# Sliding-window attention and a feed-forward layer: fp32 to fp16 in the DMA in place of on the engines

## The chip, the cores and the metric

The kernel runs on one core of a Trainium2 chip. The metric is the device time of one execution in microseconds, as the median of repeated runs. Before the change it is 325.88 us (13 runs, 324.3 to 328.38). Five engines work side by side and wait for each other by semaphores: PE (matmuls), DVE (vector), ACT (activation), Pool, and SP, which here only issues DMAs. Sixteen DMA engines move the data.

## What is computed

Attention over 8 batches, 8 heads, 576 positions and 64 dimensions, with two kinds of mask, then a feed-forward layer over the 4,608 tokens:

```python
scores = matmul(q, k.T) / sqrt(64)
rel = pos[:, None] - pos[None, :]
mask_plain = (rel >= 0) & (rel < 32)                       # heads 0 to 3
mask_dil = (rel >= 0) & (rel < 128) & (rel % 4 == 0)       # heads 4 to 7
attn = softmax(where(mask, scores, -1e9))
x = (attn @ v), all heads of a token side by side          # 4608 x 512
h = x @ w_in                                               # 512 x 2048
out = max(0.01 * h, h) @ w_out                             # 2048 x 512
```

Inputs and output are fp32. The kernel computes with fp16 operands and fp32 accumulation.

## The kernel before

**Half batches and units.** The four heads of one kind of one batch are a half batch n (0 to 15; even n are plain, odd n dilated). Each has three units u = 3n + s: s = 0 and 1 are the two pairs of heads over the first 384 positions, s = 2 is both pairs over the last 192. In the dilated kind the positions are taken by their remainder modulo 4.

**An order written out by hand.** `PROGRAM` is a list of steps; the loop at L360 executes them in this order, and each engine keeps its own share of the order. Nothing is rearranged later. The letters:

- `lq:n:p` (`load_qk`, L138) loads q and k of half batch n, pair of heads p (`b` for both), to fp32 tiles `qf`, `kf`; `lv:n` (L155) loads v to `vf`; `lw:i:g` (L316) loads a fourth of w_in (i = 0) or of w_out (i = 1), 1 MB, to `wf`. All of these are issued by SP. For n < 5 (`NPE`) q and k come as 128 rows of 2,304 bytes per pair, for the others as runs of 256 bytes.
- `cq`, `cv`, `cw` convert what was loaded to fp16 tiles (`qh`, `kh`, `vh`, `w1`, `w2`) on DVE (`V`), Pool (`P`) or ACT (`A`). `cv` makes two operations: all 128 partitions, and then 32 partitions that get a copy of the 32 rows of the tile's last quarter, for windows that begin in the tile before.
- `B:n:p` (L202), for n < 5: 18 + 18 transposes of 64x64 on PE and two copies from PSUM to `qT`, `kT`. `T:n` (L197), for the others: transposes by DMA.
- `S:u` (L241): scores of a unit into the one PSUM tile `sps`, then an exponential on ACT. `S:u:b` first adds a mask bias by two matmuls against an identity (L246); `S:u:m` doesn't, and `M:u` (L263) multiplies by a 0/1 mask on DVE instead.
- `D:u` (L272): sums (`den`) and values (`o`) on PE, then 1/sum, either by two activations on ACT (`l`) or by a reciprocal on DVE (`r`), and the product with it into the ring `xT` on DVE. With `p` its PSUM tiles come from the four-tile pool that the feed-forward uses as well.
- `I:c:j` (L334): four matmuls of the first feed-forward product for a chunk of 384 (or 192) tokens and one of 16 groups of columns, and the leaky ReLU on ACT. It needs `xT` of all heads for the chunk: units 0, 1, 3, 4 for chunk 0. `O:t:g` (L343): four matmuls of the second product for 128 tokens; after g = 3 the result is copied by ACT and stored by a DMA that ACT issues.
- `Z:m`: m warming matmuls of 512 columns that compute nothing (L392).
- `mask` builds the 0/1 mask on Pool in four operations (`band`, L102). The bias is built by the same function before the first step.

**Buffers.** `qT`, `kT` and `vh` have three buffers (`NB`), used by n modulo 3; the fp32 tiles of v have two, those of the weights three (`WF`), those of q and k two.

**The start.** Up to `I:0:0`, the first feed-forward step, PROGRAM has 35 warmers, six B (36 transposes each), eight S, six of them with the bias, and six D. From there on, I and O steps stand between the steps of attention to the end.

Of the kernel before, what the change touches and what calls it, by code (L numbers as in the profile page):

```python
# [9 lines left out]
FP16 = mybir.dt.float16  # L10
# [4 lines left out]
PAD = 128  # L15
B, H, S, D = 8, 8, 576, 64
DM = H * D
# [4 lines left out]
GRING = 1152  # L22
NEG = -30000.0
# [3 lines left out]
Z:3 lq:1:1 Z:8 lq:0:1 Z:2 cq:0:q:V:1 cq:1:k:A:1 Z:1 lq:0:0 lq:1:0 cq:1:q:P:1 lv:1:b Z:3 cq:0:k:A:1  # L27
B:1:1:VV Z:5 cq:0:q:V:0 Z:1 B:0:1:AA cq:1:k:P:0 Z:2 cq:1:q:V:0 Z:2 S:4:b B:1:0:VA lv:0:b lq:2:b
S:1:b lw:0:0 Z:1 cv:1:V:b cq:0:k:P:0 lq:3:b B:0:0:AA lw:0:1 S:3:b D:4:rp S:0:b D:3:lp cq:2:q:V:b Z:3
S:2:b Z:1 cv:0:P:b lw:0:2 D:0:lp cq:2:k:P:b D:1:l S:5:b B:2:1:AV B:2:0:VA cq:3:k:V:b Z:2 D:2:lp  # L30
cw:0:0:P lw:0:3 lv:2:b Z:1 cq:3:q:P:b S:7:m D:5:l mask S:6:m cw:0:1:V lw:1:0 I:0:0 I:0:1 M:7
B:3:0:AA S:8:m B:3:1:AV I:0:2 I:0:3 S:9:b I:0:4 cw:0:2:V I:0:5 I:0:6 M:6 I:0:7 S:11:m M:8 I:0:8
I:0:9 I:0:10 cw:0:3:V lw:1:1 I:0:11 I:0:12 I:0:13 cv:2:P:b cw:1:0:V I:0:14 I:0:15 cw:1:1:P lw:1:2
I:1:0 I:1:1 I:1:2 I:1:3 I:1:4 cw:1:2:P I:1:5 I:1:6 D:6:lp M:11 D:8:lp D:7:r S:10:m O:0:0 I:1:7 I:1:8
I:1:9 I:1:10 I:1:11 I:1:12 M:10 I:1:13 lv:3:b lw:1:3 O:1:0 O:0:1 O:1:1 cv:3:V:b I:1:14 lq:4:b O:2:0
O:2:1 cq:4:q:P:b cw:1:3:V lv:4:b lq:5:b I:1:15 cq:4:k:P:b O:0:2 D:11:l O:1:2 lq:6:b O:0:3 cq:6:q:P:b
D:10:l O:1:3 O:2:2 B:4:0:AV D:9:l B:4:1:VV S:12:m cq:5:q:V:b cq:5:k:V:b T:5 O:2:3 O:3:0 I:2:0 I:2:1
I:2:2 I:2:3 I:2:4 I:2:5 I:2:6 I:2:7 S:14:m I:2:8 I:2:9 I:2:10 I:2:11 cv:4:A:b cq:6:k:V:b O:3:1
I:2:12 lv:5:b T:6 M:14 O:3:2 I:2:13 M:12 lq:7:b O:3:3 I:2:14 lv:6:b cv:5:P:b I:2:15 I:3:0 I:3:1
I:3:2 O:4:0 I:3:3 I:3:4 S:13:m I:3:5 I:3:6 O:4:1 I:3:7 I:3:8 I:3:9 M:13 I:3:10 I:3:11 I:3:12 I:3:13  # L40
S:15:m D:12:r D:13:lp O:5:0 cq:7:q:P:b M:15 O:4:2 I:3:14 S:16:m M:16 cq:7:k:P:b T:7 lv:7:b lq:8:b
lq:9:b D:14:l O:5:1 O:4:3 S:17:m D:16:lp D:15:l I:3:15 cv:7:P:b M:17 O:5:2 O:6:0 O:6:1 I:4:0 O:5:3
I:4:1 S:19:m O:6:2 O:7:0 O:7:1 O:6:3 O:7:2 I:4:2 I:4:3 D:17:l S:20:m cq:9:k:P:b O:8:0 I:4:4 S:18:m
I:4:5 M:20 O:8:1 I:4:6 O:7:3 O:8:2 S:21:m I:4:7 cv:6:V:b I:4:8 M:18 M:19 D:20:lp S:22:m M:21 D:18:r
I:4:9 I:4:10 O:8:3 I:4:11 I:4:12 I:4:13 M:22 cq:8:k:V:b D:19:lp S:23:m D:22:lp D:21:l I:4:14 I:4:15
O:9:0 O:10:0 I:5:0 O:9:1 O:9:2 cq:8:q:V:b T:8 lv:8:b O:9:3 I:5:1 I:5:2 O:11:0 O:10:1 I:5:3 O:11:1
I:5:4 O:10:2 I:5:5 I:5:6 M:23 O:10:3 cq:9:q:P:b T:9 lq:10:b lq:11:b lv:9:b I:5:7 I:5:8 S:25:m D:23:l
I:5:9 O:11:2 I:5:10 I:5:11 I:5:12 I:5:13 I:5:14 M:25 I:5:15 I:6:0 I:6:1 O:12:0 I:6:2 O:12:1 S:26:m
O:11:3 I:6:3 I:6:4 I:6:5 cv:8:V:b I:6:6 S:28:m O:12:2 O:12:3 S:24:m cq:10:q:P:b I:6:7 I:6:8 I:6:9
O:13:0 cq:11:q:A:b I:6:10 I:6:11 O:13:1 M:28 S:27:m cq:11:k:P:b D:25:r I:6:12 I:6:13 cq:10:k:A:b  # L50
# [12 lines left out]
I:10:1 O:24:0 O:24:1 M:47 I:10:2 S:46:m I:10:3 O:24:2 I:10:4 O:25:0 S:45:m cv:15:V:b D:41:l D:47:lp
S:42:m O:25:1 I:10:5 cv:14:V:b O:25:2 I:10:6 M:42 M:46 O:24:3 I:10:7 I:10:8 M:45 I:10:9 S:43:m
D:45:lp D:46:l O:26:0 M:43 I:10:10 O:25:3 I:10:11 I:10:12 S:44:m D:43:r D:42:lp I:10:13 O:26:1
I:10:14 I:10:15 O:26:2 O:26:3 I:11:0 I:11:1 I:11:2 O:27:0 I:11:3 I:11:4 I:11:5 I:11:6 M:44 O:27:1
O:27:2 O:27:3 D:44:lp I:11:7 I:11:8 O:28:0 I:11:9 I:11:10 I:11:11 O:29:0 I:11:12 O:28:1 I:11:13
O:29:1 O:28:2 I:11:14 I:11:15 O:29:2 O:28:3 I:12:0 I:12:1 I:12:2 I:12:3 O:30:0 O:30:1 O:29:3 I:12:4
O:30:2 O:31:0 O:30:3 I:12:5 I:12:6 I:12:7 I:12:8 I:12:9 I:12:10 O:32:0 O:31:1 I:12:11 I:12:12 O:31:2
I:12:13 O:31:3 O:32:1 I:12:14 I:12:15 O:33:0 O:32:2 O:34:0 O:32:3 O:33:1 O:34:1 O:35:0 O:33:2 O:34:2  # L70
O:33:3 O:35:1 O:34:3 O:35:2 O:35:3
# [4 lines left out]
def kernel(ctx: ExitStack, tc: tile.TileContext, q, k, v, w_in, w_out, out):  # L76
# [25 lines left out]
    def band(t, one, other):  # L102
# [7 lines left out]
    band(bias, 0.0, NEG)  # L110
# [5 lines left out]
    NB = 3  # L116
# [6 lines left out]
    vf = [cst.tile([128, 24, D], FP32, name="vf0"), cst.tile([128, 32, D], FP32, name="vf1")]  # L123
    nc.vector.memset(vf[1].rearrange("p (h a r) d -> p h a (r d)", a=2, r=4)[64:128, :, 1, :], 0.0)
    nc.scalar.copy(out=vf[0][0:32].rearrange("p (a t) d -> p a (t d)", a=3),
                   in_=warm[0:32].unsqueeze(1).to_broadcast([32, 3, 512]))
    for t in kT:
        nc.vector.memset(t[:, 0:PAD], 0.0)
        nc.vector.memset(t[:, S:PAD + S], 0.0)
    nc.vector.memset(vf[1][0:32], 0.0)  # L130
# [7 lines left out]
    def load_qk(n, pairs=(0, 1)):  # L138
        b, kind = divmod(n, 2)
        base = (b * H + 4 * kind) * S * D  # L140
        for nm, x in (("q", q), ("k", k)):
            if (n, nm) not in qkf:
                qkf[n, nm] = stg.tile([128, 24, D], FP32, tag=nm + "f", name=nm + "f")
            t = qkf[n, nm]
            if n >= NPE:
                nc.sync.dma_start(t[0:96], rows_ap(x, base, [[D, 96], [96 * D, 24], [1, D]]))
            elif len(pairs) == 2:
                nc.sync.dma_start(t[:, 0:18, :].rearrange("p (a t) d -> p a (t d)", a=2),
                                  rows_ap(x, base, [[9 * D, 128], [2 * S * D, 2], [1, 9 * D]]))
            else:  # L150
                p = pairs[0]
                nc.sync.dma_start(t[:, 9 * p:9 * p + 9, :].rearrange("p t d -> p (t d)"),
                                  rows_ap(x, base + 2 * S * D * p, [[9 * D, 128], [1, 9 * D]]))

    def load_v(n, pairs=(0, 1)):  # L155
        b, kind = divmod(n, 2)
        base = (b * H + 4 * kind) * S * D
        p0, p1 = pairs[0], pairs[-1] + 1
        if kind == 0:
            nc.sync.dma_start(vf[0][32:128, 12 * p0:12 * p1, :],  # L160
                              rows_ap(v, base + 1152 * D * p0, [[D, 96], [96 * D, 12 * (p1 - p0)], [1, D]]))
        else:
            t4 = vf[1].rearrange("p (h a r) d -> p h a (r d)", a=2, r=4)
            for a, i0, w in ((0, 0, 96), (1, 96, 48)):
                nc.sync.dma_start(t4[32:32 + w, 2 * p0:2 * p1, a, :],
                                  rows_ap(v, base + (1152 * p0 + 4 * i0) * D,
                                          [[4 * D, w], [S * D, 2 * (p1 - p0)], [1, 4 * D]]))


    def cast_qk(n, nm, eng, pairs=(0, 1)):  # L170
        if (n, nm) not in qkh:
            qkh[n, nm] = att.tile([128, 24 * D], FP16, tag=nm + "h", name=nm + "h")
        t, f = qkh[n, nm], qkf[n, nm]
        for p in pairs:
# [3 lines left out]
            else:  # L178
                eng(out=t[0:96, 12 * D * p:12 * D * p + 12 * D].rearrange(  # L179
                        "p (t h d) -> p h t d", t=6, h=2),  # L180
                    in_=f[0:96, 12 * p:12 * p + 12, :].rearrange("p (h t) d -> p h t d", h=2))

    def cast_v(n, eng, pairs=(0, 1)):
        t, f = vh[n % NB], vf[n % 2]
        p0, p1 = pairs[0], pairs[-1] + 1
        if n % 2 == 0:
# [240 lines left out]
```

The softmax here doesn't subtract the row's maximum and nothing guards it: scores larger than these inputs give would overflow.

## Time and profile before

| | |
|---|---|
| median of 13 runs | 325.88 us |
| the profiled execution | 328.38 us |
| its span in the trace | 326.7 us |
| busy PE, DVE, ACT, Pool | 318.4, 130.0, 203.3, 66.5 us |
| two products of the feed-forward (L339, L349), busy PE | 139.0 and 137.3 us |
| bytes read and written in HBM | 36.70 and 9.44 MB |
| DMA engines' share of time on SP's queue | 53.4% |

The span is what the trace covers, from the first instruction to the last; the execution's own time is a little longer. The profiled execution is one of the 13 runs, and here it is the slowest of them. Busy time of PE counts each matmul from its start to a modelled end, and neighbours overlap. Start-to-start times of matmuls that follow each other tell more: 512 columns go at about 0.216 us each when the clock is full and nothing waits. "Idle before" in a line is the time that an engine stood before the instruction, with what ended that.

### The profile page before, as it was taken

Reading aid. Unit: us, or ns where it says so; the run is one execution under the profiler, and the core shown is the slowest. Engines: PE = TensorE matmul, PEld = TensorE weight load, DVE = VectorE, ACT = ScalarE, POOL = GpSimd, SP = SyncE. Lnnn points to the kernel's source line nnn. Section 1 sums busy time; section 2 is a strip of 40 time slices with the busy share of each in tenths; the row PEclk is TensorE's granted clock in tenths of the full one; section 3 lists DMA queues with packets and bytes.
Section 4 is the critical chain, followed back from the end, with each engine's and each line's share of the span. In section 5 each row is a group of like instructions: output and inputs, shape, how many; then the busy total and the mean of one; then the engine's idle time right before and its main releaser. Section 6 shows DMA issues by size and latency. Waiting matters only on the chain.

```text
span 326.7 us, 6683 instructions
## 1 busy us (share of the span) xinstructions
PE 318.4 (97%) x2809; PEld 187.3 (57%) x2809; DVE 130.0 (40%) x173; ACT 203.3 (62%) x395; POOL 66.5 (20%) x66
## 2 busy tenths in 40 slices
PE   8979999999999999999999999999999999999995
PEld 2546676566755565665546556655665555555542
DVE  4696919460360773040413392066522670000000
ACT  5487884678764684466847786656765784543412
POOL 3382445023330600015000640063000000000000
PEclk9998999999999999999999999999999999999999
DMA  7999797979969204996089969919610000001012
GB/s 247 305 407 344 279 350 222 263 171 244 184 173 286 71 32 95 240 272 109 34 208 244 221 139 229 271 40 194 162 66 1 34 34 32 32 34 64 2 65 96
DMA packets 111199, 53.06 MB, mean 162 GB/s; under 512 B 96833, under 2 KB 101441, under 8 KB 110657
## 3 DMA queue, kind: packets, MB, share of 16 engines
q1 hardware_dynamic: 105984, 43.20, 53.4%
q10 hardware_dynamic: 5184, 9.44, 7.8%
q8 instruction: 22, 0.36, 0.5%
q14 instruction: 9, 0.07, 0.1%
HBM read 36.70 MB, written 9.44 MB: 141 GB/s over the span
## 4 chain that ended last, share of the span: by engine, by line
PE 92%; DVE 2%; DMA 2%; ACT 1%; issue 1%; DVEq 0%; ACTq 0%
PE hp L339 39%; PE op L349 38%; PE sps L258 5%; PE wp L392 3%; PE den L284 3%; PE o L292 2%; DMA out_dram<-ob 2%; PE tp L209 2%; DVE rec L300 1%; DVE vh L195 1%; ACT ob L353 1%; DVE qh L176 0%; DVE vh L192 0%; ACT er L261 0%; PE sps L246 0%
## 5 line engine op out<-in xcount | busy, mean ns | idle before, releaser
L339 PE MATMUL hp<-xT,w 128*128 128x384 f16 (+1 forms) x832 | 139.0, 314 | 0.3 <-ACT ob L353 0.3
L349 PE MATMUL op<-w,gt 128*128 128x512 f16 x576 | 137.3, 379 | 0.0
L341 ACT ACTIVATE gt<-hp 128x384 f16<-128x384 f32 (+1 forms) x208 | 93.6, 466 | 56.6 <-PE hp L339 54.0
L339 PEld LDWEIGHTS <-w 128*128 128x128 f16 x832 | 89.2, 114 | 43.3 <-issue 1.3
L349 PEld LDWEIGHTS <-gt 128*128 128x128 f16 x576 | 54.6, 98 | 57.2 <-issue 0.7
L309 DVE TENSOR_TENSOR xT<-o,rec 128x384 f16<-128x384 f32 (+1 forms) x64 | 33.6, 554 | 97.1 <-ACT rec L298 95.6
L353 ACT COPY ob<-op 128x512 f32<-128x512 f32 x36 | 21.1, 585 | 38.0 <-PE op L349 36.6
L261 ACT ACTIVATE er<-sps 128x768 f16<-128x768 f32 (+1 forms) x48 | 38.6, 804 | 8.6 <-PE sps L258 7.5
L268 DVE TENSOR_TENSOR em<-er,mask 128x768 f16<-128x768 f16 (+1 forms) x41 | 28.3, 711 | 26.8 <-ACT er L261 26.4
L300 DVE RECIPROCAL rec<-den 128x384 f32<-128x384 f32 x9 | 23.0, 2552 | 19.6 <-PE den L284 19.5
L258 PE MATMUL sps<-qT,kT 64*128 64x96 f16 (+1 forms) x448 | 23.0, 229 | 0.6 <-ACT er L261 0.5
L297 ACT ACTIVATE ln<-den 128x384 f32<-128x384 f32 x39 | 18.9, 485 | 5.8 <-PE den L284 4.4
L179 POOL CAST kh<-kf 96x768 f16<-96x768 f32 x12 | 12.2, 1040 | 48.5 <-DMA kf<-in_k_dram 38.5
L258 PEld LDWEIGHTS <-kT 64*128 64x128 f16 (+1 forms) x448 | 15.2, 121 | 11.1 <-issue 9.7
L298 ACT ACTIVATE rec<-ln 128x384 f32<-128x384 f32 x39 | 20.4, 524 | 1.2
L179 POOL CAST qh<-qf 96x768 f16<-96x768 f32 x12 | 13.1, 1116 | 36.6 <-DMA out_dram<-ob 26.5
L292 PEld LDWEIGHTS <-vh 128*64 128x64 f16 (+1 forms) x448 | 15.4, 111 | 2.5
L192 POOL CAST vh<-vf 128x2048 f16<-128x2048 f32 x4 | 7.6, 1895 | 40.5 <-PE o L292 23.6
L392 PE MATMUL wp<-xT 128*128 128x512 f16 x35 | 13.0, 483 | 1.7 <-DVE xT L114 1.3
L292 PE MATMUL o<-em,vh 128*64 128x96 f16 (+1 forms) x384 | 14.3, 201 | 0.0
L284 PE MATMUL den<-em,ones 128*64 128x384 f16 (+1 forms) x82 | 14.2, 343 | 0.0
L284 PEld LDWEIGHTS <-ones 128*64 128x64 f16 (+1 forms) x96 | 5.3, 108 | 8.2 <-issue 7.4
(55 smaller groups left out, 135.5 us busy)
## 6 DMA issues: line engine op xcount, KB each, us to landing
out_dram<-ob ACTq DMA_DIRECT2D x36, 256.0 KB, 2.0
qf<-in_q_dram SPq DMA_DIRECT2D x14, 576.0 KB, 7.2
kf<-in_k_dram SPq DMA_DIRECT2D x14, 576.0 KB, 7.5
vf<-in_v_dram SPq DMA_DIRECT2D x8, 576.0 KB, 6.3
wf<-in_moe_w_in_dram SPq DMA_DIRECT2D x4, 1024.0 KB, 10.6
wf<-in_moe_w_out_dram SPq DMA_DIRECT2D x4, 1024.0 KB, 5.4
vf<-in_v_dram SPq DMA_DIRECT2D x8, 384.0 KB, 6.2
vf<-in_v_dram SPq DMA_DIRECT2D x8, 192.0 KB, 4.9
```

The costliest lines, as they stand in the source:

```text
L179: eng(out=t[0:96, 12 * D * p:12 * D * p + 12 * D].rearrange("p (t h d) -> p h t d", t=6, h=2), in_=f[0:96, 12 * p:12 * p + 12, :].rearrang ...
L258: nc.tensor.matmul(sps[0:kp, hh, w * x:w * x + w], ka, qa, start=not pe_mask, stop=not pe_mask or x == len(tiles) - 1)
L261: nc.scalar.activation(out=er[0:kp], in_=sps[0:kp, :, 0:384], func=AF.Exp, scale=SCALE)
L268: nc.vector.tensor_tensor(out=em[0:kp].rearrange("p h (t c) -> p h t c", c=w), in0=er[0:kp].rearrange("p h (t c) -> p h t c", c=w), in1=ba ...
L284: nc.tensor.matmul(den[64 * hh:64 * hh + 64, 0:384], ones[0:kp], em[0:kp, hh, :], start=True, stop=True)
L292: nc.tensor.matmul(o[64 * hh:64 * hh + 64, w * x:w * x + w], vt[0:kp, sl, :], em[0:kp, hh, w * x:w * x + w], start=True, stop=True)
L300: nc.vector.reciprocal(out=rec, in_=den[:, 0:384])
L309: nc.vector.tensor_tensor(out=out_x, in0=ins[0], in1=ins[1], op=ALU.mult)
L339: nc.tensor.matmul(hp[:, 0:w], w1[j // 4][:, i, j % 4::4], xT[:, i, x0:x0 + w], start=(i == 0), stop=(i == 3))
L341: nc.scalar.activation(out=gt[:, j, g0:g0 + w], in_=hp[:, 0:w], func=AF.Prelu, alpha=0.01)
L349: nc.tensor.matmul(op, gt[:, j, g0:g0 + 128], w2[g][:, j % 4, :], start=(j == 0), stop=(j == 15))
L353: nc.scalar.copy(out=ob, in_=op)
```

## The change

- The conversions of weights, of v, and of q and k of n < 5 leave the engines: the loads are issued by Pool (`nc.gpsimd.dma_start`) from the fp32 inputs directly into the fp16 tiles, and the DMA converts. `wf`, `vf` and the step `cw` are gone; the step `gq` takes the place of `lq` and `cq` for n < 5. q and k of n >= 5 are loaded by SP and converted on the engines as before.
- `cv` keeps only its second operation, the copy of 32 rows, now from fp16 to fp16.
- `qT`, `kT` and `vh` have four buffers in place of three; `qh` and `kh` have four (`QHB`) in place of two. The zeros that `vf` had are written to each `vh` by DVE.
- No step has `:b`: all 48 units are masked by `M` on DVE. The bias is still built, by a step of its own on Pool, and nothing reads it.
- PROGRAM is another order. Up to `I:0:0` it has 50 warmers, eight B, eight S without the bias and six D. All steps from `gq` to `lw`, and the mask, stand in one line on Pool's queue. A DMA on it also waits for the eighth DMA before it to have landed.

The diff, cut:

```diff
+QHB = 4
 PROGRAM = """
-Z:3 lq:1:1 Z:8 lq:0:1 Z:2 cq:0:q:V:1 cq:1:k:A:1 Z:1 lq:0:0 lq:1:0 cq:1:q:P:1 lv:1:b Z:3 cq:0:k:A:1
-B:1:1:VV Z:5 cq:0:q:V:0 Z:1 B:0:1:AA cq:1:k:P:0 Z:2 cq:1:q:V:0 Z:2 S:4:b B:1:0:VA lv:0:b lq:2:b
-S:1:b lw:0:0 Z:1 cv:1:V:b cq:0:k:P:0 lq:3:b B:0:0:AA lw:0:1 S:3:b D:4:rp S:0:b D:3:lp cq:2:q:V:b Z:3
-S:2:b Z:1 cv:0:P:b lw:0:2 D:0:lp cq:2:k:P:b D:1:l S:5:b B:2:1:AV B:2:0:VA cq:3:k:V:b Z:2 D:2:lp
-cw:0:0:P lw:0:3 lv:2:b Z:1 cq:3:q:P:b S:7:m D:5:l mask S:6:m cw:0:1:V lw:1:0 I:0:0 I:0:1 M:7
-B:3:0:AA S:8:m B:3:1:AV I:0:2 I:0:3 S:9:b I:0:4 cw:0:2:V I:0:5 I:0:6 M:6 I:0:7 S:11:m M:8 I:0:8
...
+Z:1 gq:0:1 Z:6 gq:3:b gq:1:0 Z:16 B:0:1:AA Z:9 gq:1:1 S:1:m lv:0:b B:3:0:AV mask B:1:0:VA Z:1
+B:3:1:AA gq:0:0 B:1:1:VV lv:1:b S:3:m gq:2:b Z:8 M:1 M:3 S:4:m Z:2 cv:0:V:b D:1:l S:5:m B:0:0:AV M:4
+S:0:m Z:1 cv:1:V:b M:0 Z:1 D:4:lp Z:1 lw:0:0 lw:0:1 D:3:lp M:5 Z:1 S:2:m M:2 lw:0:2 Z:2 D:0:l bias
+lw:0:3 B:2:0:VA B:2:1:VV lv:3:b lv:2:b S:9:m Z:1 D:5:r D:2:lp S:6:m gq:4:b I:0:0 I:0:1 lw:1:0 lw:1:3
+I:0:2 M:6 I:0:3 S:10:m I:0:4 M:10 I:0:5 S:7:m I:0:6 I:0:7 I:0:8 I:0:9 lw:1:1 I:0:10 I:0:11 I:0:12
+I:0:13 I:0:14 M:9 I:0:15 I:1:0 cv:3:V:b D:10:r S:8:m D:9:lp I:1:1 M:7 cv:2:P:b I:1:2 S:11:m M:11
+I:1:3 I:1:4 I:1:5 D:6:r I:1:6 I:1:7 I:1:8 lw:1:2 I:1:9 I:1:10 I:1:11 I:1:12 I:1:13 I:1:14 D:7:lp
+B:4:1:AA D:11:l lv:5:b lq:5:b I:1:15 I:2:0 I:2:1 I:2:2 S:13:m B:4:0:VV M:8 I:2:3 I:2:4 O:0:0 I:2:5
...
-    band(bias, 0.0, NEG)
...
-    NB = 3
+    NB = 4
...
+    for i in (1, 0, 3, 2):
+        nc.vector.memset(kT[i][:, 0:PAD], 0.0)
+        nc.vector.memset(kT[i][:, S:PAD + S], 0.0)
+        nc.vector.memset(vh[i][0:32], 0.0)
...
+    def half(n, nm):
+        if (n, nm) not in qkh:
+            qkh[n, nm] = att.tile([128, 24 * D], FP16, tag=nm + "h", bufs=QHB, name=nm + "h")
+        return qkh[n, nm]
...
+    def load_half_qk(n, pairs):
+        for nm, x in (("q", q), ("k", k)):
+            t = half(n, nm)[:, 9 * D * pairs[0]:9 * D * pairs[-1] + 9 * D]
+            nc.gpsimd.dma_start(t.rearrange("p (a r) -> p a r", r=9 * D), qk_ap(x, n, pairs))
...
+        t = vh[n % NB]
         if kind == 0:
-            nc.sync.dma_start(vf[0][32:128, 12 * p0:12 * p1, :],
-                              rows_ap(v, base + 1152 * D * p0, [[D, 96], [96 * D, 12 * (p1 - p0)], [1, D]]))
+            nc.gpsimd.dma_start(t[32:128, 12 * p0:12 * p1, :],
+                                rows_ap(v, base + 1152 * D * p0, [[D, 96], [96 * D, 12 * (p1 - p0)], [1, D]]))
...
-    def cast_v(n, eng, pairs=(0, 1)):
+    def copy_v(n, eng, pairs):
+        t = vh[n % NB]
         p0, p1 = pairs[0], pairs[-1] + 1
         if n % 2 == 0:
-            a, z = 12 * p0, 12 * p1
-            eng(out=t[:, a:z, :], in_=f[:, a:z, :])
-            eng(out=t[0:32, a + 1:z, :], in_=f[96:128, a:z - 1, :])
+            eng(out=t[0:32, 12 * p0 + 1:12 * p1, :], in_=t[96:128, 12 * p0:12 * p1 - 1, :])
...
     def load_w(i, g):
-        t = stg.tile([128, 4, 512], FP32, tag="wf", bufs=WF, name="wf")
         if i == 0:
-            nc.sync.dma_start(t, rows_ap(w_in, 512 * g, [[DFF, 128], [128 * DFF, 4], [1, 512]]))
+            nc.gpsimd.dma_start(w1[g], rows_ap(w_in, 512 * g, [[DFF, 128], [128 * DFF, 4], [1, 512]]))
...
-    def cast_w(i, g, eng):
-        eng(out=(w1, w2)[i][g], in_=wst.pop((i, g)))
...
+        elif f == "gq":
+            load_half_qk(int(a[0]), PAIRS[a[1]])
+        elif f == "bias":
+            band(bias, 0.0, NEG)
```

An even half batch's v is one DMA of 96 x 24 = 2,304 runs of 256 bytes, an odd one's two DMAs of 384 and 192 runs of 1,024 bytes. A fourth of w_in has 512 runs of 2,048 bytes, a fourth of w_out 128 of 8,192.

## The prediction

> **What bounds the kernel now.** I read the busy time by stretches first, cut at the first feed-forward matmul (L339) and at the end of the last matmul. Columns: length, then busy time and instructions of PE, PEld, DVE, ACT and POOL, granted clock, DMA share, GB/s.
>
> ```profile
> 0.00:30.03 30.03, 25.75 (x403) 13.63 (x404) 20.79 (x31) 17.67 (x27) 15.06 (x24) 0.94 0.99 335
> 30.03:323.05 293.02, 292.62 (x2410) 173.64 (x2406) 109.22 (x142) 185.04 (x368) 51.43 (x42) 1.00 0.58 145
> 323.05:326.70 3.65, 0.00 (x0) 0.00 (x0) 0.00 (x0) 0.59 (x1) 0.00 (x0) 1.00 0.31 120
> ```
>
> For 293 us PE idles 0.4 us in all: nothing that DVE, ACT, Pool or the DMA does there is late. It can only lose by this change, or gain by having fewer matmuls. The rest is the start, 30.03 us in which the DMA engines are full (share 0.99), and a tail of 3.65 us. So the question is when PE reaches the first L339, and what it has left to do then. Next the chain of waits, in order of time, and the timeline of the start.
>
> ```profile
> 8.73 0.69 PE tp L209 x36
> 24.41 2.13 PE tp L209 x72
> 26.53 0.97 PE wp L392 x2
> 310.95 12.10 PE op L349 x56
> 12.74 0.49 PE L246 MATMUL sps<-bias,ident 128*128 128x384 f16 x2
> 13.16 0.52 PE L258 MATMUL sps<-qT,kT 64*128 64x96 f16 x8
> 21.94 2.41 DVE L176 CAST qh<-qf 128x576 f16<-128x576 f32 x2
> 24.41 0.69 PE L209 MATMUL tp<-ident,qh 64*64 64x64 f16 x18 [1.42 <-DVE qh L176]
> 25.00:30.00 5.00, 4.46 (x105) 2.94 (x101) 3.06 (x7) 3.29 (x6) 1.46 (x4) 0.73 1.05 403
> ```
>
> A step B (36 transposes) costs PE 0.69 us, 512 columns 12.10 / 56 = 0.216 us, a bias pair 13.16 - 12.74 = 0.42 us. The start has 25.75 us of busy PE, 1.32 us before its first instruction and 30.03 - 25.75 - 1.32 = 2.96 us of waits, the longest 1.42 us for a cast on DVE. Soon after it the clock falls (0.73 in the last row): two B cost 2.13 us in place of 1.38 and two warmers 0.97 in place of 0.43, so the slow clock took about 1.3 us.
>
> **The change, part by part: PE.** (1) The six bias pairs in the start go: 6 x 0.42 = -2.5 us. (2) B:3:0 and B:3:1 move ahead of the first L339: +1.4 us in the start, -1.4 us after it, nothing in sum. (3) There are 50 warmers in place of 35; the added 15 come after the 17 cold ones, 15 x 0.216 = +3.2 us. (4) Half batch 3's first tile, after the start, loses its bias pair: -0.4 us. (5) If the waits of before (2.96 us) and the slow clock that followed them (1.3 us) vanish, -4.3 us. So without a single wait the first L339 would come at 30.03 - 2.5 + 1.4 + 3.2 - 4.3 = 27.8 us. The rest is 1.8 us shorter, so the span would be 326.7 - 2.2 - 1.8 = 322.7. The profiled execution took 328.38 us, 1.68 us outside its span, and is 2.50 us over the median of 325.88. Against the median the floor is 325.88 - 4.0 = 321.9 us. All that follows is waits added to it.
>
> **The casts.** They leave DVE, ACT and Pool. In the start that is worth the 1.42 us above, which (5) has already; later it is worth nothing, since PE waited 0.4 us there. The multiply by the mask, which takes the bias pairs' place (7 more, 711 ns each, on DVE), lies under PE's other steps except where a values step asks for it at once; the walk below counts those. Four buffers of q, k and v save waits that PE didn't have.
>
> **The issue on Pool.** SP issued eleven DMAs by 6.4 us. Now Pool issues 16 DMAs up to the first weights, w1[0], in one line, and each needs Pool's time. No row shows it. The rows nearest:
>
> ```profile
> 0.80 0.42 SPq L152 DMA_DIRECT2D qf<-in_q_dram  x1
> 3.68 0.66 POOL L176 CAST qh<-qf 128x576 f16<-128x576 f32 x1 [0.53 <-DMA qf<-in_q_dram]
> L189 POOL CAST vh<-vf 32x1472 f16<-32x1472 f32 x3 | 4.8, 1597 | 0.2
> L104 POOL TENSOR_SCALAR_AFFINE_SELECT mask<-mask 128x384 f16<-128x384 f16 x1 | 0.5, 530 | 0.1
> ```
>
> The low bound is SP's 0.42 us a DMA and nothing for its runs. For a program on Pool I take an issue plus one short pass of Pool, 0.42 + 0.53 = 0.95 us. A contiguous run costs one step of a Pool loop, 1597 / 1472 = 1.1 ns, or two (it has a reading and a writing side), 2.2 ns; I take 1.6. The high bound is DVE's slowest loop, the reciprocal, 2552 / 384 = 6.6 ns a run. So 128 runs cost 1.16 us, 256 cost 1.36, the 2,304 runs of an even half batch's values 4.6, the 384 and 192 of an odd one's 2.8 together, weights with 512 runs 1.8. Pool begins at 1.4 us (its identity ends there) and finishes issuing q0:1, k0:1 at 3.7, q3, k3 at 6.4, q1 and k1 at 11.0, v0 at 15.7, the mask (1.65 us, four Pool operations that stand between) at 17.3, q0:0, k0:0 at 19.6, v1 at 22.5, q2, k2 at 25.2, w1[0] at 27.0, then w1[1], w1[2], the unused bias and w1[3] at 33.9. The first load of before was usable 3.68 - 1.22 = 2.4 us after its issue; 0.7 us of this are its 0.29 MB at the 400 GB/s of that stage, the other 1.7 us are latency. I let a read of fp32 keep that rate although half as much is written.
>
> Against that PE's steps, with durations from these rows: B:0:1 at 9.9 (23 warmers, 17 of them at 0.43 us), no wait. D:1 could go at 18.0; v0 lands at 18.9 and its copy of 32 rows takes DVE 1.17 us: wait 2.1. B:0:0 at 20.8 has k0:0 at 22.1: 1.0. S:0 behind the DVE copy of kT (755 ns): 0.8. D:4 at 24.0; v1 lands at 24.7, copy 1.18: 1.8. B:2, D:5, D:2 and the first L339: 1.1 (0.14 for k2, the rest the banks that D:5's reciprocal holds). That is 6.8 us, and the first L339 is at 34.6; w1[0] to w1[3] have landed at 31.3, 33.9, 36.6 and 39.2, each before its turn (2.6 us apart from 34.6). Behind it D:6 waits 0.9 for v2, whose row copy stands on Pool behind v3 and three issues of w2, and ACT holds up I:1 for 1.0, where before lost 0.4: +1.5. Sum: 321.9 + 6.8 + 1.5 = **330.2 us**.
>
> The same walk at the low bound leaves 4.4 us before L339 (v0's and v1's copies, S:0, D:5) and 0.6 behind it, 326.9; waits that the walk finds between PE, ACT and DVE alone may not occur (down to 321.9). With 2.2 ns a run v0 holds D:1 for 4.2, v1 D:4 for 2.2 and v2 D:6 for 4.7 us, 14.8 with the rest, 336.7; with 6.6 ns the 5,440 runs up to w1[0] alone take 27 us more, beyond 350. If a packet that is cast costs as the small ones of before did (256 B in 20 ns on 16 engines, 205 GB/s), w1[0] lands near 38 and each further group 5 us later where PE needs 2.6: beyond 345.
>
> **A rule that speaks against it.** DVE's two casts of 128x576 took 2.41 us at 21.94, beside a Pool cast, and the two of k3 at 26.95, with Pool idle, 0.82 us: the two engines do hold each other up here. The Trainium skill, "SBUF — State Buffer", section "SBUF: two separate sides", goes further: while DVE copies in a mode that takes the port it shares with Pool, Pool can't write descriptors, and a DMA from its queue stands still. By this rule the two copies of v0 and v1 on DVE (1.2 us each) would delay the issues behind them, an estimate of 332.5 us in place of 330.2; no row of before has a DMA from Pool, so I leave it out of the sum.
>
> **Later in the program** Pool's one line holds the v of 14 more half batches (seven at 4.6 us, seven at 2.8, 52 us in 293) among its casts, w2, and waits for PE and DVE to free a buffer; 20 casts of q and k and eight row copies stand behind these waits. PE's steps cover all of it; without that cover a late v makes PE wait at its D step at once, since its order is fixed. I charge nothing.
>
> **The rivals.** (a) Faster, 323.3 us: Pool's issue costs no more than SP's and the 4.4 us of waits at that price shrink to 1.4 with nothing behind L339. For it: before's DVE was busy 4.97 us of the five from 15 us and 4.90 of the five from 20 us, and loses its casts there; the first pair would land 5 us before B:0:1 asks. Against: D:1 and D:4 follow their copies directly. It decides while the added waits stay under 2.4 us. (b) Within 0.5%, about 326 us: the low price with its waits (326.9), or a few of them less; the start then only trades casts for warmers. (c) The forecast, 327.5 to 335. (d) Much slower, about 341 us: 2 ns a run or more, or a slow cast in the DMA engines. For it: 256-byte runs were already the dearest in before; against: weights and q, k come in runs of 2,048 and 2,304 bytes. (e) That the casts aren't taken off the engines can't be: no instruction of that kind is left for n < 5, v and w.
>
> **How the numbers follow.** A measurement tells 0.5% (1.6 us) from nothing: below 324.3 is faster, above 327.5 slower. Chances: (a) 0.24, (b) 0.20, (c) 0.36, (d) 0.20. Faster 0.24, same 0.20, slower 0.36 + 0.20 = 0.56. The time is that of (c), 330.2, whose own range is 327.5 to 335. The range takes in (b), all of (a) but its best (down to 322.8), and half of (d), to 341.5; about 0.15 is left out.
>
> **What would show it.** The first L339 near 34.6 us; Pool's DMA rows near 1.2 us for q and k, and several times that for an even v; PE idle before L292 (D:1, D:4) and L209 (B:0:0), released by DVE copies and loads. No row of PE waiting after about 60 us, and PE idle under 3 us from the first L339 to the end. It is wrong if Pool's issues are as short as SP's, if L339 comes before 30 us, or if PE waits for weights (the DMA's rate) or for v in the middle.

## The result and the profile after

| | before | after |
|---|---|---|
| median | 326.03 us (48 runs) | 330.10 us (11 runs, 328.32 to 331.19) |
| ratio | | 1.0116, 95% interval 1.0093 to 1.0139 |
| the profiled execution, its span | 328.38, 326.7 us | 328.89, 327.2 us |
| mean granted clock in it | 0.995 | 1.000 |

The granted clock is the share of PE's full clock that the profile records. Ratios and their intervals leave out single runs more than 1.5% above the fastest of the same kernel; medians take in all runs.

The change makes the kernel 1.2% slower. The two profiles differ by far less than the medians, because neither is typical: that of before has 3.41 us at half clock in its start and lies 2.4 us above its median, that of after has none and lies 1.2 us below. Of twelve runs of after nine have a mean clock of 0.990 to 0.995 (their median is 330.2), three have 1.000 (328.3 to 329.2); two of the nine, at 0.993, are as short as those three (328.2 and 328.5). So the start of after at full clock is read from the profile, and the clock is an account of its own.

In the changed kernel L339 has become L332 (first feed-forward product), L349 L342, L258 L259 (scores), L284 and L292 L285 and L293 (D), L209 L210 (transposes), L392 L385 (warmers). The busy time by stretches, cut as it was for before, at the first L332 and at the end of the last matmul; the columns are the same:

```profile
0.00:32.05 32.05, 26.59 (x479) 14.95 (x480) 17.21 (x35) 15.87 (x26) 21.62 (x40) 1.00 1.22 191
32.05:323.62 291.57, 291.54 (x2332) 172.27 (x2331) 99.10 (x138) 179.26 (x355) 42.09 (x49) 1.00 0.62 119
323.62:327.20 3.58, 0.00 (x0) 0.00 (x0) 0.00 (x0) 0.59 (x1) 0.00 (x0) 0.98 0.32 122
```

Behind the first L332 PE idles 0.03 us in 291.6: the whole loss is in the start, 2.0 us longer than in before's profile although that one ran at half clock for a part of it. PE's first matmul comes at 1.34, so PE stood for 32.05 - 26.59 - 1.34 = 4.1 us there. Who waited for whom, on PE, up to 36 us (total, times, longest):

```profile
PE sps L259 <- issue: 1.6, 1, 1.6
PE wp L385 <- DVE xT L112: 1.3, 1, 1.3
PE sps L259 <- DVE kT L212: 0.9, 1, 0.9
PE tp L210 <- DMA kh<-in_k_dram: 0.5, 1, 0.5
PE tp L210 <- DMA qh<-in_q_dram: 0.4, 1, 0.4
PE hp L332 <- DVE kT L212: 0.3, 1, 0.3
```

The 1.3 us are the beginning. The longest wait of the start is for "issue", that is, for nothing that the profile names. It stands in the middle of a step, S:3, whose operands PE already had for its first two matmuls (timeline of PE):

```profile
16.39 0.26 PE L259 MATMUL sps<-qT,kT 64*128 64x96 f16 x2
18.26 0.43 PE L259 MATMUL sps<-qT,kT 64*128 64x96 f16 x6 [1.61 <-issue]
18.63 1.90 PE L385 MATMUL wp<-xT 128*128 128x512 f16 x8
```

Pool's line and one copy on DVE, from the timeline of after:

```profile
2.76 0.73 POOL L159 DMA_DIRECT2D qh<-in_q_dram  x1
...
6.29 1.26 POOL L167 DMA_DIRECT2D vh<-in_v_dram  x1
...
12.50 0.69 POOL L172 DMA_DIRECT2D vh<-in_v_dram  x1 [1.34 <-DMA kh<-in_k_dram]
...
20.17 0.58 DVE L193 COPY vh<-vh 32x1472 f16<-32x1472 f16 x1
```

Pool issues a DMA in 0.5 to 0.8 us, an even v in 1.26, and stands where the eighth DMA before has not landed. It is not the issue that is late but the data: v0 is issued at 6.29 and lands at 18.16, the first weights are issued at 16.24 and land at 26.42 (21.26 in before). The DMA queues up to 30 us (packets, MB, share of 16 engines' time) show who shares the engines:

```profile
q0 software_dynamic: 6699, 4.48, 100.9%
q1 hardware_dynamic: 4640, 1.18, 20.1%
q8 instruction: 3, 0.05, 0.6%
```

q0 is Pool's queue. q1 is SP's, and the 1.18 MB on it are q and k of half batch 5, whose casts start at 67 us. SP has nothing else left to issue in the start, so the step `lq:5`, late in PROGRAM, runs at 0.81 us; in before it stood behind the start's loads on the same queue and ran at 46 us. Its 256-byte packets take 0.201 x 30 = 6 us of all sixteen engines by this account, in which the times of packets in flight together overlap (the shares add up to 121%); what they cost the kernel is left to the runs.

### The profile page after: what moved, and what is told of

Read it like the earlier page. It is cut to its first block, busy times and chain, and to the rows that moved or that the text cites. A ratio compares the mean times of both kernels' runs of the same rounds, so it can differ in the third digit from the quotient of the medians.

```text
span 327.2 us, 6650 instructions
## 1 busy us (share of the span) xinstructions
PE 318.1 (97%) x2810; PEld 187.2 (57%) x2810; DVE 116.3 (36%) x172; ACT 195.7 (60%) x381; POOL 63.7 (19%) x88
## 3 DMA queue, kind: packets, MB, share of 16 engines
q1 hardware_dynamic: 77088, 19.47, 29.8%
## 4 chain that ended last, share of the span: by engine, by line
PE 91%; DMA 3%; DVE 2%; POOL 1%; ACT 1%; issue 1%; POOLq 0%
PE hp L332 39%; PE op L342 39%; PE sps L259 5%; PE den L285 4%; DMA kh<-in_k_dram 3%; PE o L293 2%; PE wp L385 1%; PE tp L210 1%; POOL qh L159 1%; DVE xT L310 0%; DVE qT L212 0%; DVE kT L212 0%; POOL kh L159 0%; ACT rec L299 0%; DVE em L269 0%
## 5 line engine op out<-in xcount | busy, mean ns | idle before, releaser
L332 PE MATMUL hp<-xT,w 128*128 128x384 f16 (+1 forms) x832 | 139.4, 314 | 0.3 <-DVE kT L212 0.3
L342 PE MATMUL op<-w,gt 128*128 128x512 f16 x576 | 137.3, 379 | 0.0
L334 ACT ACTIVATE gt<-hp 128x384 f16<-128x384 f32 (+1 forms) x208 | 94.4, 465 | 63.4 <-PE hp L332 58.2
L332 PEld LDWEIGHTS <-w 128*128 128x128 f16 x832 | 89.4, 114 | 43.4 <-issue 1.1
L342 PEld LDWEIGHTS <-gt 128*128 128x128 f16 x576 | 54.5, 98 | 57.0 <-issue 0.7
L301 DVE RECIPROCAL rec<-den 128x384 f32<-128x384 f32 x14 | 35.7, 2553 | 42.8 <-PE den L285 42.8
L269 DVE TENSOR_TENSOR em<-er,mask 128x768 f16<-128x768 f16 (+1 forms) x48 | 26.0, 567 | 24.7 <-ACT er L262 24.4
L259 PE MATMUL sps<-qT,kT 64*128 64x96 f16 (+1 forms) x448 | 23.1, 229 | 2.5 <-issue 1.6
L259 PEld LDWEIGHTS <-kT 64*128 64x128 f16 (+1 forms) x448 | 15.0, 121 | 12.4 <-issue 9.2
L298 ACT ACTIVATE ln<-den 128x384 f32<-128x384 f32 x34 | 16.6, 487 | 6.2 <-PE den L285 6.0
L299 ACT ACTIVATE rec<-ln 128x384 f32<-128x384 f32 x34 | 17.8, 523 | 1.1
L184 POOL CAST qh<-qf 96x768 f16<-96x768 f32 x10 | 8.1, 832 | 50.5 <-DMA qf<-in_q_dram 42.2
L285 PE MATMUL den<-em,ones 128*64 128x384 f16 (+1 forms) x96 | 16.9, 346 | 0.2
L293 PEld LDWEIGHTS <-vh 128*64 128x64 f16 (+1 forms) x448 | 15.6, 110 | 2.2
L293 PE MATMUL o<-em,vh 128*64 128x96 f16 (+1 forms) x448 | 16.8, 201 | 0.0
L385 PE MATMUL wp<-xT 128*128 128x512 f16 x50 | 15.2, 431 | 1.5 <-DVE xT L112 1.3
L172 POOL DMA_DIRECT2D vh<-in_v_dram x16 | 10.0, 631 | 22.6 <-PE den L285 15.9
L184 POOL CAST kh<-kf 96x768 f16<-96x768 f32 x10 | 8.1, 835 | 30.6 <-issue 16.3
L285 PEld LDWEIGHTS <-ones 128*64 128x64 f16 (+1 forms) x96 | 5.6, 107 | 10.2 <-issue 8.3
```

The lines of the kernel that those rows point to most:

```text
L259: nc.tensor.matmul(sps[0:kp, hh, w * x:w * x + w], ka, qa, start=not pe_mask, stop=not pe_mask or x == len(tiles) - 1)
L269: nc.vector.tensor_tensor(out=em[0:kp].rearrange("p h (t c) -> p h t c", c=w), in0=er[0:kp].rearrange("p h (t c) -> p h t c", c=w), in1=ba ...
L285: nc.tensor.matmul(den[64 * hh:64 * hh + 64, 0:384], ones[0:kp], em[0:kp, hh, :], start=True, stop=True)
L293: nc.tensor.matmul(o[64 * hh:64 * hh + 64, w * x:w * x + w], vt[0:kp, sl, :], em[0:kp, hh, w * x:w * x + w], start=True, stop=True)
L301: nc.vector.reciprocal(out=rec, in_=den[:, 0:384])
L332: nc.tensor.matmul(hp[:, 0:w], w1[j // 4][:, i, j % 4::4], xT[:, i, x0:x0 + w], start=(i == 0), stop=(i == 3))
```

## The experiments

Three suspects came out of this: (A) q5 and k5, loaded first instead of last; (B) the 15 added warmers; (C) scores without a bias, whose multiply on DVE is one more step between ACT and D. The first four kernels take them one at a time, and the weights alone.

**e1: hold q5 and k5 back.** Pool touches the tile before SP may load it, and reaches this in its order only at 39 us.

```diff
             t = qkf[n, nm]
+            if n == NPE:
+                nc.gpsimd.memset(t[0:1, 0, 0:1], 0.0)
             if n >= NPE:
```

> The changed kernel with SP's first loads (q and k of half batch 5, 1.18 MB in runs of 256 bytes, which SP issues at 0.8 us because nothing stands before them on its queue any more) held back until Pool has issued v of half batch 5, near 40 us, by a one-element memset of their tiles on Pool. Theory A (the loads of the start land late, and these two are in their way): k1:0 lands near 10 us in place of 14.1, v0 near 14 in place of 18.2, the first feed-forward matmul 1 to 2 us before 32.05, time 328 to 329. Theory B (the 15 added warmers and the rest of PE's own work are the cost): no change, 330.1 within 0.6.

Measured: 331.36 us (four runs, 327.81 to 332.74; 330.68 without the longest, which the ratio leaves out), ratio 1.0151 (1.0074 to 1.0227). Neither A's 328 to 329 nor B's 330.1 came, and four runs this far apart don't tell e1 from after. The loads did come sooner (k1:1 lands at 14.06 instead of 15.95, v0 at 15.93 instead of 18.16), and in the profiled run nothing of it reached the end: its first L332 (here L334) comes at 34.34. Timeline of PE and, below, the stretch from 20 to 25 us of e1:

```profile
14.98 0.26 PE L261 MATMUL sps<-qT,kT 64*128 64x96 f16 x2
18.27 0.44 PE L261 MATMUL sps<-qT,kT 64*128 64x96 f16 x6 [3.02 <-issue]
```

```profile
20.00:25.00 5.00, 4.75 (x75) 2.66 (x73) 1.39 (x4) 2.65 (x5) 3.50 (x5) 0.67 1.24 206
```

PE reached the same two matmuls of S:3 1.4 us sooner and then waited 3.02 us, to the same time as in after, 18.27 against 18.26. After this pause the clock is at half for two stretches of 3.41 us (0.67 on the mean here). What PE waits for did not move with the data.

**e2: the 15 added warmers taken out** (Z:9 to Z:5, Z:8, Z:2 and Z:1 gone).

```diff
-B:0:1:AA Z:9 gq:1:1
+B:0:1:AA Z:5 gq:1:1
...
-S:3:m gq:2:b Z:8 M:1 M:3 S:4:m Z:2 cv:0:V:b
+S:3:m gq:2:b M:1 M:3 S:4:m cv:0:V:b
...
-M:5 Z:1 S:2:m
+M:5 S:2:m
```

> The changed kernel with 15 warmers fewer after the first transposes (9 to 5, 8 to none, 2 to none, 1 to none), so 35 as in the kernel before. Theory B: 15 x 0.216 = 3.2 us less, 326.9. Theory A: PE waits for loads and copies where the warmers stood; the first feed-forward matmul moves by less than 1 us, 329.2 to 330.1, and a lower clock after the longer waits may take even that back.

Measured: 329.36 us, ratio 1.0127 (1.0092 to 1.0162); the first L332 at 32.04 as in after. Theory B falls: 3.2 us less work of PE went into a longer pause (2.2 us, to 18.00), into other waits (0.9 us for ACT, 0.5 for the copy of v0) and into 6.83 us at half clock. In this start the warmers cost next to nothing, since PE would have waited or slowed in their place.

**e3: bias in the start again** (six units `S:u:b`, no `M` for them, the bias built early on Pool and the mask later).

```diff
-S:1:m lv:0:b B:3:0:AV mask B:1:0:VA
+lv:0:b bias S:1:b B:3:0:AV B:1:0:VA
...
-S:3:m gq:2:b Z:8 M:1 M:3 S:4:m
+S:3:b gq:2:b Z:8 S:4:b
...
-S:2:m M:2 lw:0:2 Z:2 D:0:l bias
+S:2:b lw:0:2 Z:2 D:0:l mask
```

> The changed kernel with the six units of the start masked by the bias on PE again (S:b) and not by DVE; the bias is built where the mask was, the mask where the bias was. PE has 6 x 0.42 = 2.5 us more, DVE six multiplies of 0.55 us less. Theory C (the multiply stands in the chain from the exponential to D:1, D:4 and sets the start): first feed-forward matmul at 31.5 or before, 328.5 to 330. Theory B: 332.6. Theory A: the added PE work fills waits for loads in part, 330 to 331.5.

Measured: 333.19 us, ratio 1.0243 (1.0213 to 1.0272). Theory C falls: the bias doesn't make the start shorter, and the change's masking on DVE is worth keeping. The number is nearest to B's 332.6, which e2 speaks against; of the 3.1 us over after, 1.1 are a longer pause, which stands here in a bias matmul of S:3 and takes 2.7 us, and the bias pairs' own price is 2.5.

**e4: before, with only the weights loaded by Pool's queue** and converted in the DMA (the eight `cw` steps and `wf` gone).

```diff
     def load_w(i, g):
-        t = stg.tile([128, 4, 512], FP32, tag="wf", bufs=WF, name="wf")
         if i == 0:
-            nc.sync.dma_start(t, rows_ap(w_in, 512 * g, [[DFF, 128], [128 * DFF, 4], [1, 512]]))
+            nc.gpsimd.dma_start(w1[g], rows_ap(w_in, 512 * g, [[DFF, 128], [128 * DFF, 4], [1, 512]]))
```

> The kernel before with one part of the change alone: the weights are loaded and converted by Pool's DMAs, q, k and v as before, the order of the rest untouched. Theory D (a DMA that converts is dear in itself, through its packets or Pool's issues): 328 or more. Theory A: the weights lie under the feed-forward's own work, eight casts less on DVE and Pool change nothing on PE, 325.2 to 326.6.

Measured: 328.01 us, ratio 1.0081 (1.0049 to 1.0112). Not free either, and the number is theory D's. Two lines of its timeline, and then the corresponding Pool cast of before:

```profile
23.96 1.28 POOL L176 CAST kh<-kf 128x576 f16<-128x576 f32 x2 [4.12 <-DMA kf<-in_k_dram]
...
25.29 0.47 PE L209 MATMUL tp<-ident,kh 64*64 64x64 f16 x18 [1.93 <-POOL kh L176]
```

```profile
19.23 1.28 POOL L176 CAST kh<-kf 128x576 f16<-128x576 f32 x2
```

k2 lands at 23.81 instead of 18.76. In before SP issued q2 and k2 ahead of the weights; now the weights run beside them from a queue of their own (issued at 12.00 and 13.49, k2 at 13.34). PE waits 1.93 us for the cast of k2. It is A's mechanism with other transfers: what stood in line on one queue no longer does. That the 1.93 us are the whole of the 2 us was not tried apart. For D speaks only the number: Pool's issues of the weights take 0.74 to 0.88 us here, and transfers that convert land no further apart than plain ones (last section).

**A new theory, F.** The pauses of after, e1, e2 and e3 stand in different instructions, but all four after exactly 223 matmuls. The trace records fetches of 16,384 bytes on the queue called instruction: 22 of them for 2,810 matmuls with as many weight loads, so 256 instructions or 128 matmuls each. The first, with the matmul behind the 223rd:

| kernel | 223rd matmul starts | first fetch | 224th starts |
|---|---|---|---|
| before | 18.84 | 13.93 to 15.06 | 18.84 |
| after | 16.39 | 16.01 to 16.98 | 18.26 |
| e1 | 14.99 | 16.05 to 17.02 | 18.27 |
| e2 | 15.58 | 15.50 to 16.45 | 18.00 |
| e3 | 16.44 | 16.94 to 17.91 | 19.30 |

PE goes on 1.2 to 1.6 us after the fetch has ended, which points to a wait for its own instructions. The Trainium skill, "Advanced Engine Details and Errata", section "ISA Cache", states a cache line of 16 KB or 256 instructions; the size of the fetches agrees. The first fetch began 2.3 us after the 96th matmul in before and 3.6 to 3.9 us after it in the four others, all with Pool's DMAs in the start.

The next kernels test F against (G), a wait for data or for a queue that the profile doesn't name. A second profile of before stands ahead of them.

**The kernel before, once more.**

> The kernel before, unchanged, profiled once more: its first profile had 3.41 us of half clock at 24.3 us and was 2.35 us above its median. If that stretch is all of the excess, the span is 324 +-0.6, the first L339 comes at 28.0 to 28.8 us instead of 30.03, and what lies behind it is 295.5 to 296.6 us, as before. If the first profile's start was typical, the first L339 stays near 30.

Measured: 328.19 us, with the same half clock at nearly the same place (24.5 to 27.9 us), first L339 at 30.34:

```profile
20.00:25.00 5.00, 3.19 (x56) 2.00 (x56) 4.90 (x6) 4.09 (x8) 3.87 (x5) 0.95 1.05 406
25.00:30.00 5.00, 4.52 (x111) 3.14 (x110) 3.50 (x8) 2.98 (x6) 1.89 (x5) 0.71 1.06 410
```

So it is no view of a run at full clock either, and the 28.0 to 28.8 stay unseen. But the 15 plain runs beside it settle the point that matters: thirteen of them have a mean clock of 0.998 or more and a median of 325.94 us, two have 0.993 and take 327.48 and 328.09, and this one, at 0.995, took 328.19. By these the stretch costs a run of before about 2 us, though one run at full clock took 327.83 as well.

**e5: more matmuls, to remove a wait.** Each of the first 23 warmers is cut into four of 128 columns: 69 matmuls more for the same work.

```diff
+            m = 4 if len(a) > 1 else 1
+            for i in range(m * int(a[0])):
+                c = slice(512 // m * (i % m), 512 // m * (i % m) + 512 // m)
+                nc.tensor.matmul(wp[:, c], warm[:, 0:128], warm[:, c], start=True, stop=True)
...
-Z:1 gq:0:1 Z:6 gq:3:b gq:1:0 Z:16 B:0:1:AA
+Z:1:s gq:0:1 Z:6:s gq:3:b gq:1:0 Z:16:s B:0:1:AA
```

> The kernel after, with each of its first 23 warming matmuls cut into four of a quarter of the columns: 69 matmuls (138 PE instructions) more, no less work. Theory F (the 1.6 us pause inside S:3 is PE waiting for instructions: it stops after its 223rd matmul until some 1.3 us after the instruction fetch that began 3.7 us after the 96th): the 223rd matmul now falls inside B:1:0, the fetch begins about 69 matmuls sooner (near 13.5 us), PE pauses at B:1:0 for 0.5 to 1.2 us at most and no longer in S:3, which runs through by 17.5 us; first L332 (its line may move by 2) near 30.5 to 31.3, time 328.0 to 329.3. Rival G (the pause is a wait for data or for a queue that the profile does not name): the pause stays after the second matmul of S:3 and ends at 18.2 to 18.3; more matmuls cost up to 1 us; time 330 to 331.

Measured: 328.01 us (ten runs), ratio 1.0051 (1.0025 to 1.0076), an interval clear of after's. The fetch begins at 11.37, ends at 12.32, and the 224th matmul goes at 15.02 without a pause; F had the fetch near 13.5 and a short pause left. Waits of PE from 5 to 40 us, and S:3 in its timeline:

```profile
PE tp L210 <- DMA qh<-in_q_dram: 0.9, 1, 0.9
PE sps L259 <- DVE kT L212: 0.9, 1, 0.9
PE tp L210 <- DMA kh<-in_k_dram: 0.3, 1, 0.3
```

```profile
16.50 0.53 PE L259 MATMUL sps<-qT,kT 64*128 64x96 f16 x8
```

The "issue" line is gone, S:3 is whole, and the first L332 comes at 29.98 instead of 32.05. The data land as in after (k1 at 16.05 against 15.95, v0 at 18.21 against 18.16), so G has no reason for this; F is shown.

**e6 and e7: half batch 3's transposes behind the first up projections**, so that PE reaches its 223rd matmul later; e7 also holds q5 and k5 back.

```diff
-lv:0:b B:3:0:AV mask B:1:0:VA Z:1 B:3:1:AA gq:0:0
+lv:0:b Z:3 mask B:1:0:VA Z:1 Z:3 gq:0:0
...
-lv:2:b S:9:m Z:1 D:5:r
+lv:2:b Z:1 D:5:r
...
-I:0:0 I:0:1 lw:1:0 lw:1:3 I:0:2 M:6 I:0:3 S:10:m I:0:4 M:10 I:0:5 S:7:m
+I:0:0 I:0:1 B:3:0:AV lw:1:0 lw:1:3 I:0:2 B:3:1:AA M:6 I:0:3 S:9:m I:0:4 I:0:5 S:10:m I:0:6 M:10 I:0:7 S:7:m
```

> The kernel after, with the transposes of batch 3 (B:3:0 and B:3:1, 72 matmuls) moved behind the first up projection steps, six warmers in their place, S:9 moved behind them. Theory F: the 223rd matmul comes in D:1, at 18.5 us or later, when the fetch has landed or nearly: no pause over 0.5 us inside S:3; first L332 at 29.5 to 30.8 (the pause of 1.6 and B:3's own 1 us gone from the start, B:3 back behind it), time 327.3, 326.5 to 328.8. Rival G: the pause inside S:3 stays and ends at 18.2 to 18.3; time 330 or above.

> The same as the run before it, and SP's loads of q5 and k5 held back to 39 us as in the first experiment. Theory F with A (q5 and k5 take 1.5 to 2 us of the start's loads, and the first experiment showed nothing of it only because PE waited for instructions): v0 lands near 16, the 223rd matmul is reached in D:1 near 17.5, pause at most 0.8 us; first L332 at 28.5 to 29.8; time 326.0, 324.8 to 327.3. Rival G: PE pauses to 18.2 in S:3 again, time 330 to 331.5 as in the first experiment.

Measured: 329.88 us (1.0117; 1.0066 to 1.0168) and 329.02 us (1.0086; 1.0054 to 1.0119). The pause is gone in both and the first up projection comes at 29.35 and 29.08, close to F's 29.5 to 30.8 and within its 28.5 to 29.8; the times missed by 2.6 and 3.0 us. Behind that point 295.3 us follow instead of 291.6: PE is busy 2.4 us more there, with the 72 transposes and S:9, and waits 1.3 us for a normalization on DVE in front of the transposes. A step moved out of the start came back behind it, dearer.

**e8: e5 and e1 together**, split warmers and late q5 and k5.

> The split warmers of e5 and the held-back q5 and k5 of e1 together, nothing else. If the early loads of q5 and k5 cost 1.5 to 2 us that e1 could not show because PE waited for instructions (theory F with A): the fetch starts near 11.4 as in e5, so PE reaches its 223rd matmul near 13.7 without a pause; S:3 ends near 15.4 instead of 17.0; first L334 (the up projection) near 28.5 instead of 29.98; time 326.3, 325.3 to 327.3. Rival (the start is paced by PE's own work and by the copies, and the loads have nothing to give): first L334 stays at 29.5 to 30.2, time 327.7 to 328.5 as in e5.

Measured: 326.43 us (ten runs), ratio 1.0006 (0.9987 to 1.0025): after's loss is gone. Busy time by stretches, and the waits of PE from 5 to 40 us:

```profile
0.00:28.89 28.89, 26.35 (x547) 19.63 (x548) 16.99 (x34) 15.39 (x25) 21.34 (x39) 1.00 1.15 166
28.89:320.47 291.58, 291.55 (x2336) 172.34 (x2332) 99.08 (x139) 179.29 (x356) 42.08 (x51) 1.00 0.64 123
```

```profile
PE sps L261 <- DVE kT L214: 0.9, 1, 0.9
```

PE has one named wait left in the start, and the rest is as long as in after. The four kernels make a square: after 330.10, late loads alone 331.36, split warmers alone 328.01, both 326.43. The early q5 and k5 cost 1.6 us once PE has its instructions; while it lacks them, holding them back gains nothing in e1's four runs.

**e9, e10, e11: can it beat both kernels?** e9 puts B:3 in the place of the eight warmers behind S:3; e10 is e9 without nine later warmers; e11 is e8 with four warmers fewer and v0's copy earlier.

```diff
 e9 (against e8)
-B:3:0:AV mask B:1:0:VA Z:1 B:3:1:AA gq:0:0 B:1:1:VV lv:1:b S:3:m gq:2:b Z:8 M:1 M:3
+Z:3 mask B:1:0:VA Z:1 Z:3 gq:0:0 B:1:1:VV lv:1:b S:3:m gq:2:b B:3:0:AV B:3:1:AA M:1 M:3
 e10 (against e9): Z:2 behind S:4 and the Z:1, Z:2 up to S:6 are gone
 e11 (against e8)
-gq:2:b Z:8 M:1 M:3 S:4:m Z:2 cv:0:V:b D:1:l
+gq:2:b Z:4 M:1 cv:0:V:b M:3 S:4:m Z:2 D:1:l
```

> As the run before it, with the transposes of batch 3 moved behind S:3, into the place of eight warmers, and six warmers in their old place: the start keeps B:3 and loses the 1.9 us of warmers. Theory F with A: 223rd matmul near 15.3 (fetch landed by 13.6), the 351st near 20.3 against a fetch that lands by 20.9, pause of 0 to 0.6; first L334 at 28.0 to 28.8, time 325.6, 324.8 to 326.8. Rival (ACT and DVE, which copy B:3 then, become late with S:3 and D:1): first L334 at 29.5 or later, time 327.5 or above.

> As the run before it, without the nine warmers (some 2 us of PE) that stand between S:4 and S:6. If these warmers now stand on the path (PE waits for nothing there): first L334 at 26.3 to 27.3, time 324.3, 323.5 to 325.3 at full clock. Rivals: they fill waits for ACT and Pool, and the time stays at that of the run before; or the idle they leave halves the clock for 3.41 us or more, and it is 1 to 3 us longer than the run before.

> As e8 (split warmers, q5 and k5 held back), with four of the eight warmers behind S:3 taken out (4 x 0.22 = 0.9 us of PE) and the copy of v0 on VectorE ahead of M:3, so that D:1, which needs it, is ready 1 us sooner. If those warmers are on the path, now that the loads are early: D:1 near 17.8 instead of 18.7, first L334 near 28.0 instead of 28.89, time 325.5, 324.8 to 326.3, at or just below the kernel before. Rivals: S:0's wait for VectorE grows by as much, time 326.4 as in e8; or the clock drops in the start as it did in e10, time 327 or above.

Measured: 328.38 us (1.0072; 1.0045 to 1.0099), 327.14 us (1.0004; 0.9966 to 1.0041) and 326.82 us (1.0017; 0.9991 to 1.0043). None beats before. e9's rival came true (first L334 at 32.05). e10's came true in part: the first L334 comes at 29.64 and the clock is at half for 6.83 us, but the time is 1.2 us below e9's and not above it. e11 lies between its two rivals, and what its profile shows was in neither. Waits of PE in e10 and its stretch from 20 to 25 us, then the waits in e11:

```profile
PE o L295 <- DVE vh L195: 1.2, 1, 1.2
PE sps L261 <- DVE kT L214: 0.9, 1, 0.9
```

```profile
20.00:25.00 5.00, 4.15 (x96) 3.43 (x92) 3.00 (x5) 3.26 (x6) 4.32 (x6) 0.55 1.25 209
```

```profile
PE tp L212 <- issue: 1.5, 2, 1.0
```

In e9 and e10 DVE copies B:3 first and then v0, which D:1 waits for, and every run of both lost clock (0.987 to 0.995). In e11 the old wait is back, in two places. PE's 223rd matmul starts at 13.15 us, the fetch ended at 12.39, and the 224th goes at 13.89, 1.5 us after that. The 350th, 127 matmuls further, starts at 18.98, the second fetch ended at 18.71, and the 351st goes at 20.15, 1.4 us after that: F holds at the next piece, too. Five of e11's twelve runs lost clock (327.4 to 328.4 us), the other seven have a median of 326.28. The fastest single runs of e10 and e11 are 324.93 us, no better than before's own (323.96).

## Why the prediction was right, and by which terms

The time, 330.2 us against a median of 330.10, came out by terms that were wrong on both sides: a floor 2.5 us too low, waits 2.7 us too long, 1.5 us behind the start that didn't come, and 1.2 us of clock that weren't foreseen. That they cancel to 0.1 us is luck. That the start would lose time was right; how was not: of the signs that the prediction named, L332 came at 32.05 in place of 34.6, Pool's rows for q and k took 0.53 to 0.74 us in place of 1.2 or more, and PE didn't wait at D:1, D:4 or B:0:0.

- **The start decides: right.** PE stood 0.03 us behind the first L332. PE's own terms (bias, B:3, warmers) gave 27.8 us for that point without waits; busy PE and its beginning make 26.59 + 1.34 = 27.9. The rest was to be 1.8 us shorter and is 1.5 shorter, tail included.
- **The first step that failed: the floor against the median.** "Against the median the floor is 325.88 - 4.0 = 321.9 us" took the waits and the half clock of before's profile off (4.3 us), and then measured from a median that mostly lacks this half clock. The second profile and the runs beside it say that the stretch is about 2 us of the 2.50 that the profiled execution lay above the median. It was counted twice; a floor near 324.4 fits (the profiled execution less 4.0).
- **The second: Pool's issue, mis-sized.** 1.16 us for 128 runs measured 0.53 to 0.70, 1.8 for 512 runs 0.75, 4.6 for an even v 1.26; from 128 to 2,304 runs that is some 0.3 ns a run, (1.26 - 0.58) / (2304 - 128), in place of 1.6. Pool was done with its first nine DMAs at 7.5 us, not at 15.7.
- **The waits of the walk: 4.1 us in place of 6.8, and mostly others.** D:1 (2.1), D:4 (1.8) and B:0:0 (1.0) are not in the list of PE's waits at all; the copy before D:1 took 0.58 us, not 1.17. S:0 waited 0.86 for the copy of kT (0.8 foreseen). Not foreseen were the 1.61 us for instructions and 0.87 for the loads of q1 and k1, which q5 and k5 held up. Whoever moves loads off a queue has to walk that queue, too: the prediction had SP issue "eleven DMAs by 6.4 us" in before, and never asked what SP would do first after.
- **Behind L332: +1.5 foreseen, 0.03 measured.** The v on Pool's line was never late for PE.
- **Clock: no term foreseen, +1.2 us on the median.** In the profiled execution, at full clock, 324.4 + 0.1 + 4.1 + 0.3 = 328.9, which is what it took (0.1 and 0.3 by the first point). The other runs lose, by their mean clock of 0.995 or 0.990, a stretch or two of 3.41 us at half clock (3.41 / 2 is 0.5% of 328). The Trainium skill, "TensorE: Matmul & The Clock Gate", section "What's actually happening", says that the clock is set by PE's activity over windows of this length; e1, e3 and e2, with the longest pauses (3.0, 2.7 and 2.2 us), have two, one and two such stretches behind them in their profiles, and after, with 1.6 us, has none, which agrees as far as it goes. The pause is not the only way there: e9 and e10 have two without it.
- **The read at 400 GB/s: right.** The four fourths of w_in land 2.6, 2.5 and 2.7 us apart, from 26.42 to 34.26 us: 3 x 1.05 MB / 7.84 us = 401 GB/s.
- **The rule on the port that DVE and Pool share: not seen at the issues.** The copy of v1 on DVE, 24.79 to 25.46 us, lies beside the issues of v2 (1.18 us from 24.04) and q4 (0.71 from 25.21); with DVE idle an even v took 1.26 and the same kind of q or k 0.71 (15.26). The issue at 16.24, beside DVE's copies from PSUM, took 0.74, that at 22.04, with DVE idle, 0.76. The copy of v0 lies beside no issue but beside a step of the bias on Pool, which took 0.71 us where its neighbour took 0.53.

Of rival (a) the condition came true, an issue nearly as short as SP's, and the time did not: it took for granted that the data would follow the issue.

The 4.1 us between the medians are thus, by the square of e1, e5 and e8: 2.1 us for PE's wait for instructions, 1.6 for the early q5 and k5, and 0.2 to 0.4 that e8 can't tell from nothing. How much of the 2.1 is the clock behind the wait is not shown: seven of e5's ten runs lose a stretch as well. Open is why the fetch began later in after than in before. The load on the DMA engines would do it, but e5, with the same load, had it 2.7 us after the 96th matmul, at a time when other DMAs ran; no run takes these apart.

## What to carry to other kernels

When loads move to a second queue, write down the new first entries of both: what was last on the old one starts at once and competes with what is needed first, and the remaining order between the queues is lost. An "issue" wait in the middle of a step, at the same count of instructions whatever the data do, is an engine waiting for its own instructions; many small matmuls early bring it about, and shifting the count (even by adding instructions) moves it away. Set the clock of a profiled run against that of the median before the one is subtracted from the other.

## What the hardware showed that was not expected

- PE's instructions come in 16,384-byte fetches through the same DMA engines, and the places where PE can run short lie 127 matmuls apart here (behind the 223rd and the 350th); a fetch that ended at 16.98 us let PE go on at 18.26, with 1.2 to 1.6 us between the two in every pause seen.
- A packet that the DMA converts takes some 14 ns more than a plain one of the same size read (medians of after and before): 107 against 93 ns for 2,304 bytes, 98 against 84 for 2,048, 32 against 18 for 256. The transfers didn't get longer by it: an even v landed 2.2 us behind the DMA before it (15.95 to 18.16 us), in before 2.4 (12.46 to 14.81), and a fourth of w_in 2.5 to 2.7 us, in before 2.6 (26.69 to 29.26).
- Fifteen warmers, 3.2 us of PE by their own price, were worth at most 0.7 us in a start that waits: without them the profile shows 6.83 us of half clock, and the time is 329.36 us against 330.10, with intervals that overlap.
